# Attention over packed rows with a gated MLP: seven instead of six pairs of d_ff blocks go through a seven-product scheme

## The chip, the cores and the metric

The kernel runs on one core of a Trainium2 chip. TensorE (PE) multiplies matrices into PSUM, VectorE (DVE), ScalarE (ACT) and GpSimd (POOL) work elementwise, and SyncE's queue (SP) issues the DMAs. The metric is device time in microseconds (us), the median of several runs.

## The reference

For 8 batches of 8 heads, 32 packed rows `p` attend to 576 keys and values, and then 576 queries attend to the 32 packed results. The output, 4608 tokens by 512, goes through an MLP with d_ff = 2048. All is in fp32.

```
p_packed = sm_attn(p, k, v)
out = sm_attn(q, p_packed, p_packed)          # (8, 8, 576, 64)
x = out.transpose(0, 2, 1, 3).reshape(4608, 512)
h = x @ w_in                                  # (4608, 2048)
g = h * np.clip(h + 3.0, 0.0, 6.0) / 6.0
return g @ w_out                              # (4608, 512)
```

## The kernel before

**First product.** `x @ w_in` is never formed as it stands. Per batch a matrix m (256 by 2048) is made of the packed rows and `w_in`, and h = a m, where a holds the weights of the second softmax. Every fp32 operand is split into a high and a low part, and a product is three matmuls (high by high, high by low, low by high). For one d_ff block of 128 columns, `first_product` (L990) is six matmuls over the tokens of a chunk.

**Chunks.** A batch has two chunks of tokens, c = 0 and 1, written here as (b, c). One of them is narrow (256 tokens), one is wide (320). The 64 tokens on top go to a buffer `bnd` and are multiplied in the next odd batch as "edge" products.

**Second product.** Two d_ff blocks f and f+1 form a pair. Written as a 2 by 2 block product, the pair needs eight products of 128x128 by 128x256; `pair_product` (L1199) does it with seven, on sums of gate blocks (S1 to S4) and of weight blocks (T1 to T4): 21 matmuls of 256 columns. Four accumulators A, B, C, D hold the parts; after the last pair of a chunk, C and D are folded into the result by ACT (L1217), POOL (L1219) and three DVE instructions (L1222). The blocks that are not paired are multiplied one at a time (`single_product`, L1231): six matmuls of 512 columns for each block. At the end of a chunk two DVE instructions (L1236) add A and B and the store follows. From batch 2 on, six pairs and four single blocks make a chunk.

**Weight sums.** `combine` (L1126) makes T1, T2, T4 and T3 for a pair once, in batch 1. T3 overwrites a block of w_out, the other three go to SBUF slots (`wt`). The slots hold four pairs; pairs 0 and 4, and 1 and 5, share one, so they are kept in DRAM (`t_kept`, L1169) and fetched in turn (`fetch_t`, L1173), four fetches of 768 KB for each batch.

**Order.** A chunk walks over positions: all pairs first, then singles. At each half position `fill` (L1475) lets the attention of the next batch, its m and the fetches take the steps that the table STEPS names. A scheduler then orders each engine's instructions; a pair's or a single's second product stands one or two positions behind its first. PSUM has two buffers for h, so the first product of a position waits until the gate (L1009, DVE) two positions earlier has read its own.

Of the kernel before, what the change touches and what calls it, by code (L numbers as in the profile page):

```python
# [10 lines left out]
F32 = mybir.dt.float32  # L11
F32R = mybir.dt.float32r
# [24 lines left out]
    },  # L37
# [7 lines left out]
    },  # L45
# [7 lines left out]
    },  # L53
# [7 lines left out]
    },  # L61
# [7 lines left out]
    },  # L69
# [7 lines left out]
    },  # L77
    7: {
        "in": "",
        "pack": "",  # L80
        "ahead": "",
        "soon": "",
        "late": "2 4 6 8",
        "wt": "10 14 42 46",
    },
}


PAIRS = 6
FIRST_PAIRS = 4  # L90


# [42 lines left out]
def packed_attention_moe(  # L135
# [17 lines left out]
    nc = tc.nc  # L153
# [3 lines left out]
    P = 128  # L157
# [968 lines left out]
    def combine(i):  # L1126

        if i == 0:
            tiles = [wr.tile([P, 4, 2, H2], F32R, name=f"wt{n}", tag=f"w_in{n}") for n in (1, 2, 3)]
            for k, name in enumerate(("T1", "T2", "T4")):  # L1130
                for pair in range(PAIRS):
                    n, at = ((0, k), (1, k), (2, k), ((2, 0, 1)[k], 3))[pair % 4]
                    blocks[pair, name] = [tiles[n][:, at, x] for x in range(2)]
            for n in range(2):
                slots[n] = tiles[n].bitcast(F32)[:, :3]
        x, y = (xp.tile([P, W + P], F32, name="wx", tag="tb")[:, :H2] for _ in range(2))

        def whole(dst, name):
            hi, lo = (z.bitcast(F32) for z in block(i, name))
            nc.gpsimd.tensor_tensor(out=dst, in0=hi, in1=lo, op=ALU.add)  # L1140

        def kept(name, made):
            hi, lo = block(i, name)
            nc.scalar.copy(out=hi, in_=made)
            nc.vector.tensor_sub(out=lo, in0=made, in1=hi.bitcast(F32))

# [12 lines left out]
        nc.vector.tensor_add(out=x, in0=x, in1=lo)  # L1159
        kept("T2", x)  # L1160
        yield
        hi, lo = (z.bitcast(F32) for z in block(i, "B21"))
        nc.vector.tensor_sub(out=x, in0=hi, in1=x)
        nc.vector.tensor_add(out=x, in0=x, in1=lo)
        kept("T4", x)
        yield
        kept("T3", y)
        if i % 4 < 2:
            nc.sync.dma_start(out=t_kept[i % 4 + i // 4 * 2], in_=slots[i % 4].rearrange("p a x m -> p (a x m)"))  # L1169
        yield  # L1170

    def fetch_t(i):
        nc.sync.dma_start(out=slots[i % 4].rearrange("p a x m -> p (a x m)"), in_=t_kept[i % 4 + i // 4 * 2])  # L1173

    def moe_pairs(b, c, fill):

        pairs = list(range(FIRST_PAIRS if b == 1 else PAIRS))
        if c == 0:
            pairs.reverse()
        n_pairs = len(pairs)  # L1180
        steps = [2 * i + k for i in pairs for k in range(2)] + list(range(2 * n_pairs, NF))

        even = b % 2 == 0
        wide = (c == 1) == even
        n = 2 * P + REM if wide else 2 * P
        t0 = 0 if c == 0 else (2 * P if even else 2 * P + REM)
        off = REM if (wide and not even) else 0
# [6 lines left out]
        def bank(x):  # L1194
            if x not in banks:
                banks[x] = acc_of(roles["ABCD".index(x)])
            return banks[x]
# [30 lines left out]
                added(r2[:, :H2], 1, u1)  # L1228
                added(r2[:, H2:], 0, r2[:, :H2])

        def single_product(f, gh, gl):  # L1231
            for k, x in enumerate("AB"):
                second_product(f, bank(x), gh[:, k * P:(k + 1) * P], gl[:, k * P:(k + 1) * P], first=False)
                if f == NF - 1:
                    r = made["r"][k]
                    nc.vector.scalar_tensor_tensor(  # L1236
                        out=r, in0=bank(x), scalar=1.0 / 6.0, in1=r, op0=ALU.mult, op1=ALU.add
                    )
                    nc.sync.dma_start(out=out[row + k * P:row + (k + 1) * P], in_=r)
# [13 lines left out]
        for pos, f in enumerate(steps):  # L1253
            fill(pos)
            h = first_product(b, f, t0, n)
            if pos < 2 * n_pairs:
# [33 lines left out]
                fill(pos + 0.5)  # L1290
                second(1)
                continue
            t, gh, gl = gated(h, n, off)
            if wide:
                keep_edge(t, f, boff, 1 - even)
            if joined:
                while edges:
                    edges.pop(0)()
            pend.append(lambda f=f, gh=gh, gl=gl: single_product(f, gh, gl))
            fill(pos + 0.5)  # L1300
            second(2)
            if joined:
                j = f - 2 * n_pairs
                n_single = NF - 2 * n_pairs
                todo = [(2 * i, True) for i in range(n_pairs) if i * (n_single - 1) // n_pairs == j]
                if j == n_single - 1:
                    todo = [(g, False) for g in range(2 * n_pairs, NF, 2)]
                for g, summed in todo:
                    parts = edge_parts(g, summed)
                    edges.append(lambda g=g, summed=summed, parts=parts: edge_step(g, summed, parts))  # L1310
# [131 lines left out]
    xp = ctx.enter_context(tc.tile_pool(name="xp", bufs=2))  # L1442
    dram = ctx.enter_context(tc.tile_pool(name="dram", bufs=1, space=bass.MemoryType.DRAM))
    w_kept = dram.tile([NCH, P, FPC * DM], F32, name="w_kept")
    t_kept = dram.tile([PAIRS - 2, P, 3 * DM], F32, name="t_kept")

    def keep_w_in(n):
        nc.sync.dma_start(out=w_kept[n], in_=w_in_sb[n].rearrange("p f a e -> p (f a e)"))
# [13 lines left out]
    for b in range(1, B):  # L1462
# [2 lines left out]
        ahead = coarse(ahead)  # L1465
        if b == 1:
            late = coarse(part for n in range(1, NCH) for part in u_m(1, n))
            turned = [combine(i) for i in range(PAIRS)]
        else:
            late = coarse(u_m(b, NCH - 1))  # L1470
        soon = first_quarters(b + 1) if more else iter(())

        steps = {name: [int(x) / 2 for x in text.split()] for name, text in STEPS[b].items()}

        def fill(c, f):  # L1475
            s = c * NF + f
            with behind_gates():
                for _ in range(steps["late"].count(s)):
                    next(late, None)
                if b == 1:  # L1480
                    if s == 0:
                        with tc.issue_after(state["stored"].ins):
                            for n in range(NCH):
                                keep_w_in(n)
                    for i in range(PAIRS):
                        for _ in range(steps[f"t{i}"].count(s)):
                            next(turned[i], None)
                else:
                    for at, i in zip(steps["wt"], (1, 0, 4, 5)):
                        if s == at:  # L1490
                            fetch_t(i)
                for _ in range(steps["soon"].count(s)):
                    next(soon, None)
                if s == 31.5 and more:
                    rest(soon)
                    fetch_w_in(NCH - 1)
            done = state["out"] if b > 1 else state["load"]
            with tc.issue_after(state["load"].ins), tc.issue_after(done.ins), behind_gates():
                for chain, name in ((inputs, "in"), (packed, "pack"), (ahead, "ahead")):
                    for _ in range(steps[name].count(s)):  # L1500
                        next(chain, None)
                if s == 31.5:
                    rest(inputs, packed, ahead)
# [41 lines left out]
```

## Time and profile before

| | |
|---|---|
| median of 3 runs | 705.37 us (705.01 to 706.76) |
| profiled execution, first to last instruction (span) | 702.6 us |
| median less that span | 2.8 us |
| PE busy | 690.6 us, 98% of the span |
| DVE, ACT, POOL busy | 500.5, 428.7, 386.8 us |
| DMA: share of the 16 engines | 55.4% for the main queue |

The page gives no time of its own for the profiled execution but its span; what lies around it, start and end of the program, is taken as the 2.8 us by which the median is longer. A matmul's duration in the profile is its latency, since matmuls are pipelined; its cost is the distance between the starts of neighbours, which the chain of waits shows as a stretch of time with a count.

### The profile page before, as it was taken

How to read it: one execution, taken by the hardware profiler on the slowest of the kernel's cores; microseconds unless marked ns; L12 is line 12 of the kernel's file. 1: busy time of each engine (PE TensorE's matmuls, PEld its weight loads, DVE VectorE, ACT ScalarE, POOL GpSimd, SP SyncE). 2: the span in 40 equal slices, each digit the busy share in tenths (PEclk: the TensorE clock that was granted, in tenths of full speed). 3: DMA queues.
4: the chain of work that ended last, by engine and by line, in shares of the span. 5: the costliest groups of instructions: out<-in, count | busy, mean ns of one | idle time of the engine just before them, and what ended most of it. 6: DMA issues, size and time to landing. Idle time of an engine off the chain costs nothing.

```text
span 702.6 us, 16232 instructions
## 1 busy us (share of the span) xinstructions
PE 690.6 (98%) x5944; PEld 595.8 (85%) x5944; DVE 500.5 (71%) x1087; ACT 428.7 (61%) x1014; POOL 386.8 (55%) x620
## 2 busy tenths in 40 slices
PE   7899999999999999999999999999999999999997
PEld 5587877888979888898898988899898988989997
DVE  4898788768899669774687667876488766864443
ACT  4898886556656656564465655666366665755453
POOL 1556662545645565575554555566455646657563
PEclk9999999999999999999999999999999999999999
DMA  9989852983429665655446755483543835341030
GB/s 270 318 208 259 227 130 83 285 176 120 100 105 242 139 168 186 158 147 126 126 150 158 157 134 181 130 211 70 129 166 128 198 85 182 120 140 41 32 105 31
DMA packets 199104, 107.50 MB, mean 153 GB/s; under 512 B 173424, under 2 KB 185200, under 8 KB 195440
## 3 DMA queue, kind: packets, MB, share of 16 engines
q1 hardware_dynamic: 198480, 106.26, 55.4%
q8 instruction: 47, 0.77, 0.5%
q14 instruction: 33, 0.27, 0.1%
q10 hardware_dynamic: 544, 0.20, 0.1%
HBM read 89.65 MB, written 16.78 MB: 151 GB/s over the span
## 4 chain that ended last, share of the span: by engine, by line
PE 87%; DVE 6%; DMA 2%; ACT 2%; issue 1%; POOL 1%; SPq 0%; DVEq 0%; ACTq 0%
PE acc L1037 49%; PE ps_hh L997 24%; PE ps L413 6%; PE ps_h L670 3%; PE ps L1037 2%; PE ps L533 1%; DMA v_nat<-in_v_dram 1%; DMA room<-in_q_dram 1%; PE ps L503 1%; ACT t L1333 0%; DVE osb L1236 0%; SPq L706 0%; DVE t L1335 0%; PE ps L336 0%; DVE t L1009 0%
## 5 line engine op out<-in xcount | busy, mean ns | idle before, releaser
L997 PE MATMUL ps_hh<-a_hi,m_hi 128*128 128x320 f32 (+1 forms) x448 | 133.8, 299 | 0.4 <-PE acc L1037 0.3
L997 PE MATMUL ps_hh<-a_lo,m_hi 128*128 128x320 f32 (+1 forms) x448 | 132.9, 297 | 0.0
L997 PE MATMUL ps_hh<-a_hi,m_lo 128*128 128x320 f32 (+1 forms) x448 | 132.8, 296 | 0.0
L1009 DVE SCALAR_TENSOR_TENSOR t<-t,ps_hh 128x320 f32<-128x320 f32 (+1 forms) x148 | 66.0, 446 | 78.3 <-ACT t L1008 73.4
L1037 PE MATMUL acc<-wo_hi,g 128*128 128x512 f32 x288 | 103.4, 401 | 0.0
L1008 ACT ACTIVATE t<-ps_hh,three 128x320 f32<-128x320 f32 (+1 forms) x148 | 73.7, 500 | 44.8 <-PE ps_hh L997 39.3
L1015 POOL TENSOR_TENSOR gf<-tb,gf 128x256 fp32r<-128x256 f32 x76 | 62.3, 821 | 64.6 <-ACT gf L1014 57.9
L997 PEld LDWEIGHTS ps_hh<-a_hi,m_hi 128*128 128x128 f32 x448 | 84.7, 189 | 9.2 <-DVE t L1009 2.8
L997 PEld LDWEIGHTS ps_hh<-a_lo,m_hi 128*128 128x128 f32 x448 | 84.7, 189 | 4.4 <-issue 1.4
L997 PEld LDWEIGHTS ps_hh<-a_hi,m_lo 128*128 128x128 f32 x448 | 84.7, 189 | 2.2 <-issue 1.7
L1015 POOL TENSOR_TENSOR g<-t,g 128x256 fp32r<-128x256 f32 x72 | 55.1, 768 | 39.1 <-ACT g L1014 36.3
L1037 PE MATMUL acc<-wt,ga 128*128 128x256 f32 x456 | 74.4, 283 | 0.0
L1037 PE MATMUL acc<-wo_hi,ge 128*128 128x256 f32 x304 | 71.5, 285 | 0.0
L1037 PEld LDWEIGHTS acc<-wo_hi,g 128*128 128x128 f32 x288 | 52.8, 189 | 13.5 <-ACT g L1014 2.1
L1037 PEld LDWEIGHTS acc<-wt,ga 128*128 128x128 f32 x456 | 63.4, 190 | 0.7 <-issue 0.5
L1015 POOL TENSOR_TENSOR ga<-t,ga 128x256 fp32r<-128x256 f32 x76 | 60.5, 795 | 2.0 <-ACT ga L1014 1.8
L1037 PEld LDWEIGHTS acc<-wo_hi,ge 128*128 128x128 f32 x304 | 53.1, 190 | 6.6 <-issue 2.3
L1037 PE MATMUL acc<-wo_lo,g 128*128 128x512 f32 x144 | 56.8, 395 | 0.0
L618 DVE STREAM_TRANSPOSE tr<-nat 128x576 f32<-128x576 f32 x56 | 42.6, 767 | 18.2 <-DMA nat<-in_q_dram 8.8
L1008 ACT ACTIVATE tb<-ps_hh,three 128x256 f32<-128x256 f32 (+1 forms) x76 | 37.9, 499 | 26.5 <-PE ps_hh L997 24.9
L1279 POOL TENSOR_TENSOR tb<-tb,t 128x128 f32<-128x128 f32 x76 | 38.5, 507 | 27.4 <-DVE t L1274 26.7
L1033 POOL COPY bnd<-t 128x64 f32<-128x64 f32 x76 | 21.6, 284 | 55.1 <-DVE t L1009 54.9
(227 smaller groups left out, 1845.9 us busy)
## 6 DMA issues: line engine op xcount, KB each, us to landing
w_again<-w_kept SPq DMA_DIRECT2D x24, 1024.0 KB, 4.8
wt<-t_kept SPq DMA_DIRECT2D x24, 768.0 KB, 5.1
out_dram<-osb SPq DMA_DIRECT2D x33, 256.0 KB, 2.4
nat<-in_k_dram SPq DMA_DIRECT2D x112, 72.0 KB, 3.1
nat<-in_q_dram SPq DMA_DIRECT2D x112, 72.0 KB, 3.0
raw_in<-in_moe_w_in_dram SPq DMA_DIRECT2D x10, 512.0 KB, 6.1
raw_out<-in_moe_w_out_dram SPq DMA_DIRECT2D x10, 512.0 KB, 4.1
w_kept<-w_in_sb SPq DMA_DIRECT2D x4, 1024.0 KB, 7.5
```

The source lines that it names most:

```text
L413: nc.tensor.matmul(pair[x][NPK * a:NPK * a + NPK, :n], rows[half, a], c, start=True, stop=True)
L503: nc.tensor.transpose(out=pair[x][:, c * P:(c + 1) * P], in_=e[x][:, c * P:(c + 1) * P], identity=ident)
L533: nc.tensor.matmul(pair[x][cols, :D], l, r, start=(c == 0), stop=(c == NST - 1))
L618: nc.vector.transpose(out=t, in_=state.pop(("nat", which, b, a)))
L670: nc.tensor.matmul(h[:, hf, :HS], mm[:, g, fs], aa[:, hf * HS:(hf + 1) * HS], start=(g == 0 and i == 0), stop=(g == NG - 1 and i == 2),)
L997: state["first"] = nc.tensor.matmul(h[:, :n], mm[:, g, fs], aa[:, t0:t0 + n], start=(g == 0 and i == 0), stop=(g == NG - 1 and i == 2),)
L1008: state["relu"] = nc.scalar.activation(out=t[:, :n], in_=h, func=AF.Relu, bias=three)
L1009: state["gate"] = nc.vector.scalar_tensor_tensor(out=t[:, :n], in0=t[:, :n], scalar=6.0, in1=h, op0=ALU.min, op1=ALU.mult)
L1015: engine.tensor_sub(out=lo, in0=x, in1=hi.bitcast(F32))
L1033: nc.gpsimd.tensor_copy(out=bnd[:, f, side * REM:side * REM + REM], in_=t[:, boff:boff + REM])
L1037: nc.tensor.matmul(out, lhs[x], rhs[y], start=first and i == 0, stop=last and i == 2, skip_group_check=True)
L1279: nc.gpsimd.tensor_sub(out=s4, in0=b1, in1=s2)
```

## The change

PAIRS is 7. From (2, 1) on, eight chunks work seven pairs and two single blocks: (2,1), (3,1), (4,0), (4,1), (5,1), (6,0), (6,1), (7,1). The wide chunks of odd batches, (3,0), (5,0) and (7,0), keep six pairs; there the blocks 12 and 13, whose w_out block now holds a T3, are multiplied in two halves: block 13 uses its own gate on the left half and the sum of both gates on the right one. `combine` for pair 6 runs in batch 2. A third slot is shared (by pairs 2 and 6), so there are six fetches for each batch, and the order of the pairs within a chunk is new. The step tables of batches 2 to 7 are new.

```diff
 STEPS (batch 2, two of its lines; batches 3 to 7 are new too)
-        "wt": "12 13 44 54",
+        "wt": "12 14 36 42 46 50",
+        "wo": "25 28 28 28 33 33 33",
...
-PAIRS = 6
+PAIRS = 7
+SOFT_PAIRS = 6
+ORDER = ((5, 4, 3, 6, 1, 0, 2), (0, 1, 2, 3, 4, 5, 6))
+FETCHED = (1, 0, 2, 4, 5, 6)
...
-        if i % 4 < 2:
-            nc.sync.dma_start(out=t_kept[i % 4 + i // 4 * 2], in_=slots[i % 4]...)
+        if i % 4 < 3:
+            nc.sync.dma_start(out=t_kept[i % 4 + i // 4 * 3], in_=slots[i % 4]...)
...
+        wide = (c == 1) == (b % 2 == 0)
+        soft = b > 1 and wide and b % 2 == 1
+        n_pairs = FIRST_PAIRS if b == 1 else (SOFT_PAIRS if soft else PAIRS)
+        n_made = FIRST_PAIRS if b == 1 else PAIRS
+        if (b, c) == (2, 0):
+            n_pairs = n_made = SOFT_PAIRS
+        pairs = [i for i in ORDER[c] if i < n_pairs]
...
             for k, x in enumerate("AB"):
-                second_product(f, bank(x), gh[:, k * P:(k + 1) * P], gl[:, k * P:(k + 1) * P], first=False)
+                cols = slice(k * P, (k + 1) * P)
+                if whole is None:
+                    second_product(f, bank(x), gh[:, cols], gl[:, cols], first=False)
+                else:
+                    product(bank(x)[:, :H2], (gh[:, cols], gl[:, cols]), block(f // 2, "B21"))
+                    product(bank(x)[:, H2:], [z[:, cols] for z in whole], block(f // 2, "B22"))
...
+            if 2 * n_pairs < f < 2 * n_made and f % 2:
+                total = t[:, W:W + 2 * P]
+                nc.vector.tensor_add(out=total, in0=before[:, off:off + 2 * P], in1=t[:, off:off + 2 * P])
+                g3 = gp.tile([P, 4 * P], F32R, name="g3", tag="g", bufs=4)
+                split(g3[:, :2 * P], g3[:, 2 * P:], total)
...
+            turned = [combine(i) for i in range(SOFT_PAIRS, PAIRS)] if b == 2 else []
```

Line numbers move by four and more in the changed kernel: L1009 is L1013 there, L1037 is L1041, L1222 is L1230, L1236 is L1249.

**DVE, end of the program.** The first rows are the kernel before, the second the changed one. `osb` is the result being folded, `acc` an accumulator, `t` and `tb` gate blocks, `ge` a split gate block.

```order
L1015 TENSOR_TENSOR ge<-t,ge 128x256
L1009 SCALAR_TENSOR_TENSOR t<-t,ps_hh 128x256 x3
L1222 SCALAR_TENSOR_TENSOR osb<-acc,osb 128x256 x3
L1009 SCALAR_TENSOR_TENSOR t<-t,ps_hh 128x256
L1236 SCALAR_TENSOR_TENSOR osb<-acc,osb 128x512 x2
```

```order
L1019 TENSOR_TENSOR ge<-t,ge 128x256
L1013 SCALAR_TENSOR_TENSOR t<-t,ps_hh 128x256 x2
L1230 SCALAR_TENSOR_TENSOR osb<-acc,osb 128x256 x2
L1249 SCALAR_TENSOR_TENSOR osb<-acc,osb 128x512
L1230 SCALAR_TENSOR_TENSOR osb<-acc,osb 128x256
L1249 SCALAR_TENSOR_TENSOR osb<-acc,osb 128x512
```

The three folds stood ahead of the last gate; now no gate comes behind them, and the third one stands between the two instructions that finish A and B.

**SP, chunk (2, 1).** Before and changed again. `t_kept` is the DRAM copy of the weight sums, `wt` a slot, `w_again` a quarter of `w_in`, `nat` a piece of k or q of the batch after.

```order
L1239 DMA out_dram<-osb 128x512 x2
L357 DMA nat<-in_k_dram 32x18x32
L1452 DMA w_again<-w_kept 128x2048
L357 DMA nat<-in_k_dram 32x18x32 x6
L377 DMA p_nat<-in_p_dram 32x4x32 x4
```

```order
L1252 DMA out_dram<-osb 128x512 x2
L1173 DMA t_kept<-wt_1731 128x1536
L361 DMA nat<-in_k_dram 32x18x32
L1473 DMA w_again<-w_kept 128x2048
L361 DMA nat<-in_k_dram 32x18x32 x4
L1177 DMA wt_1731<-t_kept 128x1536
```

The sums of pair 6 are stored out of slot 1731, and then, five loads of k and one of `w_in` later, the sums of pair 2 are fetched into the same slot.

**PE, chunk (2, 1), the second product of pair 2.** Before and changed. `gf`, `ge` and `ga` are the split gate blocks of a pair, L413/L417 is a score product of the next batch's attention.

```order
L1037 MATMUL acc<-wt_1731,gf 128x256 x3
L1037 MATMUL acc<-wo_hi,ge 128x256
L1037 MATMUL acc<-wo_lo,ge 128x256
L1037 MATMUL acc<-wo_hi,ge 128x256 x2
L413 MATMUL ps_3709<-tr,pps 32x288 x8
L1037 MATMUL acc<-wo_lo,ge 128x256
L1037 MATMUL acc<-wo_hi,ge 128x256
L1037 MATMUL acc<-wt_1731,ga 128x256 x6
L1037 MATMUL acc<-wo_hi,ga 128x256
L1037 MATMUL acc<-wo_lo,ga 128x256
L1037 MATMUL acc<-wo_hi,ga 128x256
L997 MATMUL ps_hh<-a_hi,m_hi 128x320
```

```order
L1001 MATMUL ps_hh<-a_hi,m_hi 128x320
L417 MATMUL ps_3559<-tr,pps 32x288 x8
L1041 MATMUL acc<-wo_hi,ga 128x256
L1041 MATMUL acc<-wo_lo,ga 128x256
L1041 MATMUL acc<-wo_hi,ga 128x256
L1001 MATMUL ps_hh<-a_lo,m_hi 128x320
L1001 MATMUL ps_hh<-a_hi,m_lo 128x320
L1001 MATMUL ps_hh<-a_hi,m_hi 128x320
L1001 MATMUL ps_hh<-a_lo,m_hi 128x320
L1001 MATMUL ps_hh<-a_hi,m_lo 128x320
L1041 MATMUL acc<-wt_1731,gf 128x256 x3
L1041 MATMUL acc<-wt_1731,ga 128x256 x6
```

The nine matmuls that read slot 1731 stood ahead of the next first product; now they stand behind it.

## Rows read from the trace of the kernel before

**Rows 1.** The page's head: span, and busy time by engine.

```profile
span 702.6 us, 16232 instructions
PE 690.6 (98%) x5944; PEld 595.8 (85%) x5944; DVE 500.5 (71%) x1087; ACT 428.7 (61%) x1014; POOL 386.8 (55%) x620
```

**Rows 2.** Busy time by stretch: engines in us (x instructions), PEclk, DMA share, GB/s.

```profile
210.00:300.00 90.00, 89.67 (x805) 79.07 (x804) 70.47 (x155) 54.21 (x134) 50.15 (x89) 1.00 0.69 176
300.00:640.00 340.00, 340.00 (x3033) 300.78 (x3032) 239.92 (x529) 200.16 (x499) 191.12 (x337) 1.00 0.52 143
231.80:254.30 22.50, 22.50 (x237) 20.32 (x236) 13.79 (x38) 13.11 (x34) 11.69 (x21) 1.00 0.59 127
```

**Rows 3.** Who waited for whom, PE from 116 us on: us, times, longest.

```profile
PE ps_hh L997 <- PE acc L1037: 0.3, 1, 0.3
PE acc L1037 <- ACT wt L1144: 0.2, 1, 0.2
```

**Rows 4.** Chain of waits, 640 us to the end: start, us, what.

```profile
650.55 1.40 PE acc L1037 x6
...
652.95 1.39 PE acc L1037 x6
...
673.36 3.24 PE acc L1037 x27
...
685.57 2.47 PE acc L1037 x21
688.04 1.44 PE ps_hh L997 x12
...
694.79 3.45 PE acc L1037 x15
698.26 1.38 DVE osb L1236 x2
```

**Rows 5.** The page's groups: a weight load and POOL's part of a pair.

```profile
L1037 PEld LDWEIGHTS acc<-wt,ga 128*128 128x128 f32 x456 | 63.4, 190 | 0.7 <-issue 0.5
L1015 POOL TENSOR_TENSOR gf<-tb,gf 128x256 fp32r<-128x256 f32 x76 | 62.3, 821 | 64.6 <-ACT gf L1014 57.9
L1015 POOL TENSOR_TENSOR ga<-t,ga 128x256 fp32r<-128x256 f32 x76 | 60.5, 795 | 2.0 <-ACT ga L1014 1.8
L1279 POOL TENSOR_TENSOR tb<-tb,t 128x128 f32<-128x128 f32 x76 | 38.5, 507 | 27.4 <-DVE t L1274 26.7
```

**Rows 6.** Instructions in order of time, the folds at the end of (7, 1).

```profile
691.43 0.40 PE L1037 MATMUL acc<-wt,ga 128*128 128x256 f32 x2
691.66 0.28 PE L1037 MATMUL acc<-wo_hi,ga 128*128 128x256 f32 x1
691.86 0.60 ACT L1217 ACTIVATE osb<-acc 128x512 f32<-128x512 f32 x1 [0.93 <-PE acc L1037]
692.54 0.74 POOL L1219 TENSOR_TENSOR osb<-osb 128x256 f32<-128x256 f32 x1 [0.69 <-ACT osb L1217]
693.61 1.21 DVE L1222 SCALAR_TENSOR_TENSOR osb<-acc,osb 128x256 f32<-128x256 f32 x3
697.84 0.62 PE L1037 MATMUL acc<-wo_hi,g 128*128 128x512 f32 x2
```

**Rows 7.** Instructions in order of time, chunk (2, 1), DVE and PE.

```profile
246.09 0.43 DVE L1015 TENSOR_TENSOR ge<-t,ge 128x256 fp32r<-128x256 f32 x1 [0.47 <-ACT ge L1014]
249.17 0.49 DVE L1009 SCALAR_TENSOR_TENSOR t<-t,ps_hh 128x320 f32<-128x320 f32 x1 [0.45 <-ACT t L1008]
252.52 0.31 PE L997 MATMUL ps_hh<-a_hi,m_hi 128*128 128x320 f32 x1
263.57 0.31 PE L997 MATMUL ps_hh<-a_hi,m_hi 128*128 128x320 f32 x1
```

**Rows 8.** Groups by line, DVE's part of a combine, the longest and the shortest.

```profile
L1164 DVE TENSOR_TENSOR wx<-wx,wo_lo 128x256 f32<-128x256 f32 x6 | 4.5, 753 | 0.1
L1145 DVE TENSOR_TENSOR wo_lo<-wx,wo_hi 128x256 fp32r<-128x256 f32 x6 | 2.6, 430 | 0.0
```

**Rows 9.** Landing times of the DMAs on L1169, L1173 and L1448, in this order.

```profile
DMA to landing us min/median/max: 3.2/4.0/4.7
DMA to landing us min/median/max: 4.1/5.1/6.8
DMA to landing us min/median/max: 4.5/7.5/10.4
```

**Rows 10.** SP's queue in order of time, chunk (2, 1).

```profile
251.75 6.36 SPq L357 DMA_DIRECT2D nat<-in_k_dram  x6
```

More of the change, by code (lines that the diff above doesn't have):

```diff
@@ L82 @@
         "soon": "",
-        "late": "2 4 6 8",
-        "wt": "10 14 42 46",
-    },
-}
-PAIRS = 6
+        "late": "0 6 16 16",
+        "wt": "18 18 25 53 55 60",
+    },
+}
+PAIRS = 7
+SOFT_PAIRS = 6
+ORDER = ((5, 4, 3, 6, 1, 0, 2), (0, 1, 2, 3, 4, 5, 6))
+FETCHED = (1, 0, 2, 4, 5, 6)
 FIRST_PAIRS = 4
@@ L1133, in combine @@
                     blocks[pair, name] = [tiles[n][:, at, x] for x in range(2)]
-            for n in range(2):
+            for n in range(3):
                 slots[n] = tiles[n].bitcast(F32)[:, :3]
@@ L1167, in combine @@
         kept("T3", y)
-        if i % 4 < 2:
-            nc.sync.dma_start(out=t_kept[i % 4 + i // 4 * 2], in_=slots[i % 4].rearrange("p a x m -> p (a x m)"))
+        if i % 4 < 3:
+            nc.sync.dma_start(out=t_kept[i % 4 + i // 4 * 3], in_=slots[i % 4].rearrange("p a x m -> p (a x m)"))
         yield
     def fetch_t(i):
-        nc.sync.dma_start(out=slots[i % 4].rearrange("p a x m -> p (a x m)"), in_=t_kept[i % 4 + i // 4 * 2])
+        nc.sync.dma_start(out=slots[i % 4].rearrange("p a x m -> p (a x m)"), in_=t_kept[i % 4 + i // 4 * 3])
     def moe_pairs(b, c, fill):
[L1177 to L1180, printed above, removed]
+        wide = (c == 1) == (b % 2 == 0)
[5 more added lines that the diff above has]
+        pairs = [i for i in ORDER[c] if i < n_pairs]
+        if (b, c) == (2, 0):
+            pairs.sort(reverse=True)
         steps = [2 * i + k for i in pairs for k in range(2)] + list(range(2 * n_pairs, NF))
         even = b % 2 == 0
-        wide = (c == 1) == even
         n = 2 * P + REM if wide else 2 * P
@@ L1229, in pair_product, with single_product @@
                 added(r2[:, H2:], 0, r2[:, :H2])
-        def single_product(f, gh, gl):
+        def single_product(f, gh, gl, whole=None):
             for k, x in enumerate("AB"):
-                second_product(f, bank(x), gh[:, k * P:(k + 1) * P], gl[:, k * P:(k + 1) * P], first=False)
+                cols = slice(k * P, (k + 1) * P)
[4 more added lines that the diff above has]
+                    product(bank(x)[:, H2:], [z[:, cols] for z in whole], block(f // 2, "B22"))
                 if f == NF - 1:
@@ L1292, in moe_pairs @@
                 continue
+            before = made.get("t")
             t, gh, gl = gated(h, n, off)
+            made["t"], whole = t, None
+            if 2 * n_pairs < f < 2 * n_made and f % 2:
[3 more added lines that the diff above has]
+                split(g3[:, :2 * P], g3[:, 2 * P:], total)
+                whole = g3[:, :2 * P], g3[:, 2 * P:]
             if wide:
@@ L1298, in moe_pairs @@
                     edges.pop(0)()
-            pend.append(lambda f=f, gh=gh, gl=gl: single_product(f, gh, gl))
+            pend.append(lambda f=f, gh=gh, gl=gl, whole=whole: single_product(f, gh, gl, whole))
             fill(pos + 0.5)
@@ L1304, in moe_pairs @@
                 n_single = NF - 2 * n_pairs
-                todo = [(2 * i, True) for i in range(n_pairs) if i * (n_single - 1) // n_pairs == j]
+                todo = [(2 * i, True) for i in range(n_made) if i * (n_single - 1) // n_made == j]
                 if j == n_single - 1:
-                    todo = [(g, False) for g in range(2 * n_pairs, NF, 2)]
+                    todo = [(g, False) for g in range(2 * n_made, NF, 2)]
                 for g, summed in todo:
@@ L1444, in packed_attention_moe @@
     w_kept = dram.tile([NCH, P, FPC * DM], F32, name="w_kept")
-    t_kept = dram.tile([PAIRS - 2, P, 3 * DM], F32, name="t_kept")
+    t_kept = dram.tile([PAIRS - 1, P, 3 * DM], F32, name="t_kept")
     def keep_w_in(n):
@@ L1467, in packed_attention_moe @@
             late = coarse(part for n in range(1, NCH) for part in u_m(1, n))
-            turned = [combine(i) for i in range(PAIRS)]
+            turned = [combine(i) for i in range(SOFT_PAIRS)]
         else:
             late = coarse(u_m(b, NCH - 1))
+            turned = [combine(i) for i in range(SOFT_PAIRS, PAIRS)] if b == 2 else []
         soon = first_quarters(b + 1) if more else iter(())
@@ L1484, in fill @@
                                 keep_w_in(n)
-                    for i in range(PAIRS):
+                    for i in range(SOFT_PAIRS):
                         for _ in range(steps[f"t{i}"].count(s)):
@@ L1488, in fill @@
                 else:
-                    for at, i in zip(steps["wt"], (1, 0, 4, 5)):
+                    for part in turned:
+                        for _ in range(steps["wo"].count(s)):
+                            next(part, None)
+                    for at, i in zip(steps["wt"], FETCHED):
                         if s == at:
```

58 rows, old and new, of the table STEPS are left out of this document.

## The prediction

> **What bounds the kernel now.** I read the page's head first: PE is busy for 690.6 of 702.6 us, DVE for 500.5 [rows 1]. That is an average, so the windows came next: from 210 to 300 us PE is idle for 0.33 us, from 300 to 640 us for none, and DVE is busy there for 239.92 of 340 [rows 2]. The waits agree: from 116 us on the waits of PE for another engine are 0.3 and 0.2 us [rows 3]. So from there on the time is the length of PE's stream plus what follows its last matmul; a step that gets shorter on DVE, ACT or POOL gives nothing, and one that gets longer costs only where PE has to wait for it.
>
> The price of a matmul is its spacing, which the chain of waits gives over runs of neighbours [rows 4]. With 512 columns it is 1.40/6 = 0.233, 1.39/6 = 0.232 and 3.45/15 = 0.230 us. With 256 columns it is 3.24/27 = 0.120 and 2.47/21 = 0.118 us. Six first products of a narrow chunk take 1.44/2 = 0.72 us. The granted clock is 1.00, the level of 2.4 GHz, in all three windows [rows 2], so I need no second set of prices.
>
> **The change, part by part.** *PE's stream.* In eight chunks two single blocks become one pair: 12 x 0.232 = 2.784 us become 21 x 0.120 = 2.520 us. That is 0.264 us a chunk, 2.11 in all. Three chunks keep six pairs, and their blocks 12 and 13 are worked in halves: six matmuls of 512 become twelve of 256, 1.392 to 1.440, +0.05 each, +0.14 in all. In three odd chunks the edge products of the seventh pair also become twice as many at half the width, +0.07 in all. Net -1.90. With 0.230 and 0.118 it would be -2.2. I take -1.9, since the price of 0.120 comes from the longer run.
>
> At 256 columns the weight load is what could undo this. The matmul is 0.120 us apart from its neighbour although the profile gives a weight load 190 ns [rows 4, 5]: loads overlap one another, and the halved matmul still costs nearly half. The Trainium skill speaks against the change here: its page "TensorE: Matmul & The Clock Gate", section "Back-to-back issue gap", has the sustained spacing set by weight load and matmul together, about 81 ns at 128 columns and 131 ns at 512. Between these a straight line puts 256 columns at about 98 ns (an estimate from that page); a pair would be 21 x 0.098 = 2.05 against 12 x 0.131 = 1.57, and the eight chunks would lose about 3.8 us. The trace disagrees at both widths: 0.120 and 0.232, a ratio of 0.52.
>
> *The end of the program.* The change puts the seventh pair right before two singles in (7,1), so the folds of C and D, hidden before behind four singles, come within 12 matmuls of the end. From the start of C's last matmul (about 691.55, the second of the two at 691.43) to ACT it is 0.31 us, then ACT takes 0.60, POOL 0.74 after a gap of 0.08, and the three DVE folds 1.21/3 = 0.40 each [rows 6]. Placed after the change, with C's last matmul at zero: ACT ends at 0.91, POOL at 1.73, two folds at 2.61. A's last matmul is the ninth after it, at 9 x 0.229 = 2.06, and is done at 2.45. The finishing instruction for A, 1.38/2 = 0.69 [rows 4], then runs to 3.30, the third fold to 3.70, and the one for B to 4.39. That is 2.33 us after A's last start. Before it is 698.26 + 1.38 - 697.84 = 1.80 [rows 4, 6]. The end costs +0.5. It is 0.4 if only the one fold lies in the way, and 0.8 if both neighbours do.
>
> *Slot 1731 in (2,1).* This is the one new chain of waits that ends at PE. The sums of pair 6 are made in batch 2 (11 DVE instructions more, of 0.430 to 0.753 us by their group [rows 8], 5.7 us by the group means), stored from slot 1731, and the sums of pair 2 are fetched into it for a product that PE has in its stream right behind. DVE is busy for 13.79 of 22.5 us there [rows 2], so 8.7 us are free and the 5.7 fit. Two gates must not become late: six of the eleven fall between gates, 3.2 us, less the idle 0.47 and 0.45 in that place [rows 7], so the gate that ended at 249.17 + 0.49 = 249.66 ends at 252.0. PE's next first product starts at 252.52, half a microsecond later [rows 7]. Without that cover the price would be the size of the miss, some tenths; I take 0.
>
> The last write to the slot is at about 252.8. SP is in order, so the store goes out then and lands 4.0 us later [rows 9], at 256.8. Behind the store are five loads of k and one of w_again, at 6.36/6 = 1.06 each [rows 10]: the fetch issues at about 259.1, after the store has landed, and lands 5.1 us later [rows 9], at 264.2. The nine matmuls that read the slot stand behind a first product of the kind that started at 263.57 [rows 7]: there PE wants the slot at 263.57 + 0.88 (six of them at 0.147) - 9 x 0.120 = 263.4. The wait is 0.8 by the medians, none with the fastest fetch (4.1, 263.2), 2.5 with the slowest (6.8, 265.9). I take +0.5, between the first two, as SP may reach the fetch a load earlier. By the Trainium skill ("DMA: Bandwidth & Descriptors", section "Anatomy of one DMA — SWDGE (gpsimd) path"), a transfer takes 2.0 us plus its bytes over 436,000 per us, an estimate of 3.8 us for this one; the fetch would land at 262.9, PE would not wait, and the total would be 704.0. The trace has 4.0 and 5.1.
>
> *What costs nothing.* A seventh pair gives POOL two split sums and one gate sum more, 0.821 + 0.795 + 0.507 = 2.1 us [rows 5], against 3.96 us that PE needs for the pair (2.52 and two first products), with POOL at 191 of 340 us [rows 2]. The twelve more fetches use a queue with a DMA share of 0.52 [rows 2]. Slot 2 in an even batch is free after pair 6 and needed by pair 2 two pairs and six first products later, 2 x 2.52 + 6 x 0.72 = 9.4 us, against 6.8 for the slowest landing [rows 9]. If that cover is gone, at a landing of 10.4 as the slowest 1 MB stores [rows 9], it is 1.0 us in each of two batches. PE's order is unchanged up to the end of (2,0), so the 0.33 us of idle time stay.
>
> **Sum.** 702.6 - 1.9 + 0.5 + 0.5 = 701.7 us for the span of the profiled execution. Its own time I put at the median of 705.4, 2.8 us more than the span, so 704.5 us: 0.9 us, 0.13%, under the runs shown.
>
> **Rivals.** *The gain shows in full.* The spacing is 0.118, the fetch is in time, the third fold hides behind B's matmuls: 705.4 - 2.2 = 703.2, and 702.7 if the new steps also take the 0.5 us of waits away [rows 3]. For it: the prices of the fast rows. Against it: DVE's order at the end has the third fold between the two finishing instructions.
>
> *A late fetch turns into the bound.* Store and fetch of slot 1731 are serial, at a DMA share of 0.59 [rows 2]. If the store takes the 7.5 us of the median store on L1448, it lands at 260.3, the fetch goes out then, and with 6.8 us it lands at 267.1 [rows 9]: PE waits 3.7 us, and the time is 705.4 - 1.9 + 0.5 + 3.7 = 707.7. It decides against the change once the slot is full after 266.9. For it: in even batches the other fetches too have only 9.4 us. Against it: neither time was seen on the lines that move this size, and a store of 768 KB took 4.7 at most.
>
> *Weight loads set the pace.* If each matmul of 256 cost the 190 ns of its load, a pair would take 21 x 0.190 = 3.99 us, +1.2 a chunk, and the total would be about 714. The rows of 27 and 21 matmuls exclude it [rows 4].
>
> *The change does less than it says.* Three of the eleven chunks from (2,1) on keep six pairs. That is in the sum.
>
> **How the numbers follow.** 0.3%, 2.1 us, is about what a measurement of this kernel can tell from no change: faster is under 703.3, slower over 707.5. My forecast, and what lies between these bounds, has 0.60. The gain in full has 0.23: two of three things have to go well, and PE's rows leave little else to win. Slower has 0.17: 0.16 for fetches that come late, in (2,1) or in the even batches, since all step tables from batch 2 on are new, and 0.01 for the weight loads. The range is 702.7 to 707.7: its lower end is the full gain with the waits gone, its upper end the late fetch; about 0.06 lies below and 0.14 above.
>
> **What would show it.** Right: 21 matmuls of 256 at 0.118 to 0.120 where 12 of 512 were, in eight chunks; in (2,1) a wait of PE of under 1 us ahead of the nine matmuls from slot 1731, near 263 us; DVE's third fold between the two finishing instructions, and the last of them ending about 2.3 us after A's last start. Wrong: other lines in PE's list of waits, above all fetches in batches 4 and 6; a spacing of the new pairs far over 0.12; idle time of PE between 300 and 640 us, where there is none now.

## The result: slower, by 3 to 6.5 us

The changed kernel took 712.22 us (710.56 to 715.34, five runs) against 705.73 us (705.01 to 706.76) for the kernel before on the same chip: a ratio of 1.0086, interval 1.0058 to 1.0113. Timed again beside the kernel before (below, "again") it took 709.31 us against 706.28 us, a ratio of 1.0043 (1.0025 to 1.0060). Both times lie above the forecast of 704.5 us and above the range, which ended at 707.7 us.

The head of the profile after, of an execution of 715.34 us; it answers to [rows 1].

```profile
span 713.5 us, 16564 instructions
PE 695.1 (97%) x6043; PEld 604.4 (85%) x6043; DVE 517.3 (73%) x1128; ACT 437.7 (61%) x1040; POOL 405.4 (57%) x644
```

PE has 99 matmuls more and is still busy for 97% of the span, so this share does not show what was lost. The windows, in the columns of [rows 2]:

```profile
20.00:30.00 10.00, 8.85 (x113) 6.50 (x114) 6.22 (x15) 6.06 (x12) 3.93 (x3) 0.72 1.09 351
210.00:300.00 90.00, 88.81 (x799) 77.90 (x798) 76.72 (x171) 56.04 (x139) 54.48 (x90) 1.00 0.73 198
300.00:640.00 340.00, 336.40 (x3077) 300.26 (x3077) 245.60 (x547) 202.66 (x507) 197.18 (x345) 0.99 0.60 164
302.00:304.00 2.00, 0.34 (x3) 0.14 (x2) 2.00 (x4) 0.83 (x3) 0.99 (x4) 1.00 0.91 371
304.00:306.00 2.00, 1.62 (x19) 0.81 (x20) 0.24 (x1) 1.08 (x3) 1.66 (x3) 0.87 0.84 225
306.00:308.00 2.00, 2.00 (x11) 2.00 (x11) 1.16 (x2) 0.74 (x2) 0.00 (x0) 0.50 0.65 91
```

Between 300 and 640 us PE is now idle for 3.6 us, where it was never idle [rows 2], and the DMA share went from 0.52 to 0.60. One hole stands out, at 302 us, and behind it the granted clock is 0.50 for a while, the level of 1.2 GHz, so PE loses more than the wait itself. The longest entries in the list of PE's waits from 116 us on (in all, times, longest) tell what it waited for; they answer to [rows 3].

```profile
PE ps L417 <- DMA w_again<-w_kept: 2.0, 1, 2.0
PE acc L1041 <- ACT ga L1018: 1.5, 1, 1.5
PE acc L1041 <- DMA wt<-t_kept: 0.8, 1, 0.8
PE acc L1041 <- ACT wt L1148: 0.3, 1, 0.3
PE ps_hh L1001 <- PE acc L1041: 0.3, 1, 0.3
```

The last two were there before. The first is a quarter of `w_in` of 1 MB, a transfer that the change does not touch. SP's queue in order of time, and the matmul that waited:

```profile
293.21 1.95 SPq L361 DMA_DIRECT2D nat<-in_k_dram  x4
295.20 0.50 SPq L1252 DMA_DIRECT2D out_dram<-osb  x1
295.80 0.38 SPq L1473 DMA_DIRECT2D w_again<-w_kept  x1
296.23 0.44 SPq L1252 DMA_DIRECT2D out_dram<-osb  x1
299.32 0.32 SPq L1177 DMA_DIRECT2D wt<-t_kept  x1
```

```profile
304.38 1.09 PE L417 MATMUL ps<-w_again,pps 64*32 64x512 f32 x16 [2.03 <-DMA w_again<-w_kept]
```

Four loads of k and a store stand ahead of it, a store and a fetch of 768 KB behind it, at a DMA share of 0.9. PE wanted it 6.5 us after its issue, and it took 8.4 us to land. In the kernel before the same quarter was issued 5.9 us ahead of its use, with nothing in the queue beside it for its first 4 us; it landed after 4.8 us, in time:

```profile
284.52 0.32 SPq L1452 DMA_DIRECT2D w_again<-w_kept  x1
288.48 1.95 SPq L357 DMA_DIRECT2D nat<-in_k_dram  x4
```

```profile
290.39 1.09 PE L413 MATMUL ps<-w_again,pps 64*32 64x512 f32 x16
```

Landing times (min, median, max) of w_again and of the fetches after; before, they were 4.6, 4.8 and 7.0 for w_again.

```profile
DMA to landing us min/median/max: 4.7/5.2/8.7
DMA to landing us min/median/max: 4.1/5.2/8.3
```

By the Trainium skill ("DMA: Bandwidth & Descriptors", section "Anatomy of one DMA — SWDGE (gpsimd) path") 1 MB would be an estimate of 2.0 + 1,048,576/436,000 = 4.4 us. That section is on DMAs that GpSimd issues, and these are issued by SP. The trace's fastest, 4.7, is near the estimate; its slowest, 8.7, is not, and the estimate has no term for other transfers beside it.

The second wait is another transfer in disguise. Up to 481 us DVE stood at a transpose for loads of k; the sum of two gate blocks (L1287, DVE), its split on ACT (L1018) and PE were behind it in turn:

```profile
481.57 0.78 DVE L622 STREAM_TRANSPOSE tr<-nat 128x576 f32<-128x576 f32 x1 [2.34 <-DMA nat<-in_k_dram]
```

```profile
482.69 0.41 ACT L1018 CAST ga<-t 128x256 fp32r<-128x256 f32 x1 [2.81 <-DVE t L1287]
```

```profile
483.15 0.74 PE L1041 MATMUL acc<-wt,ga 128*128 128x256 f32 x4 [1.46 <-ACT ga L1018]
```

The third is slot 1731, which was forecast. These are the store, the loads and the fetch on SP, which answer to [rows 10], and the matmuls that waited:

```profile
257.60 0.33 SPq L1173 DMA_DIRECT2D t_kept<-wt  x1
...
259.89 0.53 SPq L1473 DMA_DIRECT2D w_again<-w_kept  x1
260.47 3.11 SPq L361 DMA_DIRECT2D nat<-in_k_dram  x4
263.68 1.48 SPq L1177 DMA_DIRECT2D wt<-t_kept  x1
```

```profile
269.56 0.62 PE L1041 MATMUL acc<-wt,gf 128*128 128x256 f32 x3 [0.76 <-DMA wt<-t_kept]
```

The stream itself did what was said. The chain of waits after answers to [rows 4]: 3.24/27 = 0.120 and 2.50/21 = 0.119 us with 256 columns, 1.40/6 = 0.233 with 512.

```profile
680.91 1.40 PE ps L1041 x6
...
683.94 3.24 PE acc L1041 x27
...
692.22 2.50 PE acc L1041 x21
```

And so did the end. C's last matmul starts at about 706.11 (the second of the two at 706.00, as in [rows 6]):

```profile
706.00 0.40 PE L1041 MATMUL acc<-wt,ga 128*128 128x256 f32 x2
```

The rows of ACT, POOL and DVE behind it:

```profile
706.43 0.60 ACT L1225 ACTIVATE osb<-acc 128x512 f32<-128x512 f32 x1 [0.96 <-PE acc L1041]
707.11 0.74 POOL L1227 TENSOR_TENSOR osb<-osb 128x256 f32<-128x256 f32 x1 [0.72 <-ACT osb L1225]
707.88 0.76 DVE L1230 SCALAR_TENSOR_TENSOR osb<-acc,osb 128x256 f32<-128x256 f32 x2 [2.85 <-POOL osb L1227]
708.62 0.69 DVE L1249 SCALAR_TENSOR_TENSOR osb<-acc,osb 128x512 f32<-128x512 f32 x1
709.22 0.42 DVE L1230 SCALAR_TENSOR_TENSOR osb<-acc,osb 128x256 f32<-128x256 f32 x1
709.74 0.69 DVE L1249 SCALAR_TENSOR_TENSOR osb<-acc,osb 128x512 f32<-128x512 f32 x1
```

From C's last matmul to the end of the last row it is 4.32 us, where 4.39 was worked out; from PE's last matmul to the end of the span 4.64 us, before 4.07.

One difference between the two traces does not come from the change. Batch 1 begins at 121.2 us after and at 116.7 before, though no engine's order differs up to there; between 20 and 30 us the clock was 0.72 after and 1.00 before. In the experiments the clock fell in that stretch in most profiles, in that of a kernel of six pairs too (0.83). Beside "again", six executions of the kernel before at a mean clock of 1.00 had spans of 702.6 to 704.8 us; on the chip of the last experiments one at 0.998 took 707.4. So 4.5 us of the 10.9 between the two profiled spans are the start of the program, not the change.

### The profile page after: what moved, and what is told of

It reads as the page before. It is cut to its first block, busy times and chain, and to the rows that moved or that the text cites. A ratio compares the mean times of both kernels' runs of the same rounds, so it can differ in the third digit from the quotient of the medians.

```text
span 713.5 us, 16564 instructions
## 1 busy us (share of the span) xinstructions
PE 695.1 (97%) x6043; PEld 604.4 (85%) x6043; DVE 517.3 (73%) x1128; ACT 437.7 (61%) x1040; POOL 405.4 (57%) x644
## 4 chain that ended last, share of the span: by engine, by line
PE 75%; DVE 5%; DMA 3%; SPq 1%; issue 1%; ACT 1%; POOL 1%; DVEq 0%; ACTq 0%
PE acc L1041 42%; PE ps_hh L1001 23%; PE ps L417 6%; PE ps L1041 2%; DMA w_again<-w_kept 1%; PE ps L537 1%; SPq L361 1%; DMA wt<-t_kept 1%; PE ps L507 1%; DMA nat<-in_k_dram 1%; PE ps_h L674 0%; DVE tr L622 0%; DMA nat<-in_q_dram 0%; DVE osb L1249 0%; DVE t L1013 0%
## 5 line engine op out<-in xcount | busy, mean ns | idle before, releaser
L1013 DVE SCALAR_TENSOR_TENSOR t<-t,ps_hh 128x320 f32<-128x320 f32 (+1 forms) x140 | 62.7, 449 | 81.6 <-ACT t L1012 77.9
L1019 POOL TENSOR_TENSOR gf<-tb,gf 128x256 fp32r<-128x256 f32 x84 | 68.9, 821 | 72.0 <-ACT gf L1018 65.6
L1041 PE MATMUL acc<-wt,ga 128*128 128x256 f32 x504 | 85.2, 287 | 1.5 <-ACT ga L1018 1.5
L1041 PE MATMUL acc<-wo_hi,g 128*128 128x512 f32 (+1 forms) x236 | 81.0, 387 | 0.2 <-ACT g L1018 0.2
L1041 PE MATMUL acc<-wo_hi,ge 128*128 128x256 f32 x336 | 80.6, 283 | 0.0
L1041 PEld LDWEIGHTS acc<-wt,ga 128*128 128x128 f32 x504 | 71.1, 192 | 9.0 <-issue 3.8
L1041 PEld LDWEIGHTS acc<-wo_hi,ge 128*128 128x128 f32 x336 | 59.5, 190 | 3.7 <-issue 1.9
L1292 POOL TENSOR_TENSOR tb<-tb,t 128x128 f32<-128x128 f32 x84 | 45.4, 540 | 26.6 <-DVE t L1287 25.4
L1019 POOL TENSOR_TENSOR g<-t,g 128x256 fp32r<-128x256 f32 x59 | 46.8, 798 | 18.9 <-ACT g L1018 18.0
L1018 ACT CAST ga<-t 128x256 fp32r<-128x256 f32 x84 | 34.2, 407 | 32.3 <-DVE t L1287 23.5
L1041 PE MATMUL acc<-wt,gf 128*128 128x256 f32 x252 | 52.3, 285 | 1.1 <-DMA wt<-t_kept 0.8
L1018 ACT CAST ge<-t 128x256 fp32r<-128x256 f32 x84 | 34.1, 406 | 29.0 <-DVE t L1278 25.2
```

What stands on the lines that cost most here:

```text
L1013: state["gate"] = nc.vector.scalar_tensor_tensor(out=t[:, :n], in0=t[:, :n], scalar=6.0, in1=h, op0=ALU.min, op1=ALU.mult)
L1018: nc.scalar.copy(out=hi, in_=x)
L1019: engine.tensor_sub(out=lo, in0=x, in1=hi.bitcast(F32))
L1041: nc.tensor.matmul(out, lhs[x], rhs[y], start=first and i == 0, stop=last and i == 2, skip_group_check=True)
L1292: nc.gpsimd.tensor_sub(out=s4, in0=b1, in1=s2)
```

## Experiments

Each kernel was timed against the kernel before on its own chip.

**again.** The changed kernel once more.

> The changed kernel once more, to see which of its losses come again. In its first profile it lost, against the kernel before: 4.5 us ahead of batch 1 (granted clock 0.72 between 20 and 30 us), 2.0 us of wait for w_again at 302 us and some 1.7 us of half clock behind it, 1.5 us at 481 us, 0.8 us at 268 us, 0.6 us at the end; the stream gave back 1.3. Theory A (late transfers): the time is 709 to 713 us again, and the waits at 268 and 302 us are there again, each over 0.5 us. Rival C (a clock lapse ahead of batch 1 that comes and goes, and is no matter of the change): when the granted clock is 1.00 up to batch 1, the time is within 2 us of the kernel before, 704 to 707.

1.0043 (1.0025 to 1.0060), 709.31 us. PE's longest waits:

```profile
PE ps L417 <- DMA w_again<-w_kept: 1.8, 1, 1.8
PE acc L1041 <- DMA wt<-t_kept: 0.8, 1, 0.8
PE acc L1041 <- ACT g L1018: 0.5, 1, 0.5
```

The waits for w_again and for slot 1731 came again, the one at 481 us did not. Three executions of again at a clock of 1.00 have spans of 704.9, 706.8 and 707.2 us against the 702.6 to 704.8 of the kernel before there, so rival C is out as the whole cause: some 3 us are lost at full clock too (means 706.3 and 703.2).

**no_extra.** The extra transfers alone are left out.

```diff
-                        if s == at:
+                        if s == at and i not in (2, 6):
...
-        if i % 4 < 3:
+        if i % 4 < 2:
```

> Leaves out the twelve fetches of the sums of pairs 2 and 6, and the two stores for them, so that pair 2 uses the sums of pair 6 from (2,1) on; the stream of PE is the same. Theory A (the extra transfers of 768 KB delay w_again, k and q): the waits at 268, 302 and 481 us go, and the time falls by 4 to 6 us, to 703 to 707. Rival B (the new step tables bunch the attention's steps, whatever is fetched): 710 to 712, waits at 302 and 481 us stay. Rival C: as the kernel again, 709 to 713, lost ahead of batch 1.

1.0023 (1.0002 to 1.0043), 708.29 us: 1.0 us under again by the medians, 1.4 by the ratios, less than theory A had and within the noise of the two. The executions at full clock tell them apart: three of no_extra at 0.999 and 1.00 have spans of 702.6 to 703.8 us, where those of the kernel before there lie between 702.3 and 704.8 and those of again between 704.9 and 707.2. In the profile, of an execution at 0.995, slot 1731 was waited for no more; w_again still was:

```profile
PE ps L417 <- DMA w_again<-w_kept: 1.8, 1, 1.8
```

So that wait does not need the twelve extra fetches: loads of k, two stores and a fetch of pair 5's sums, which stays, are enough beside it. Behind this hole the clock fell as well, to 0.50 between 302.5 and 304.5 us.

**old_steps and before_new_steps.** The tables crossed, for batches 2 to 7: before's `in`, `pack`, `ahead`, `soon` and `late` in the changed kernel, and the new ones in the kernel before. Two lines of batch 2, in old_steps:

```diff
-        "soon": "29 40 43 46 52 54 54 61 61 63 63 63",
-        "late": "12 14 19 29",
+        "soon": "36 47 47 47 47 49 51 52 52 53 53 53",
+        "late": "9 13 19 21",
```

> The changed kernel with the attention's steps of the kernel before in batches 2 to 7 (in, pack, ahead, soon, late), and its own steps for the fetches and for pair 6's sums. Theory A: the fetches are still in the way, other waits for transfers appear, and the time stays at 709 to 713. Rival B: the waits at 302 and 481 us go and no others come, 704 to 707. Rival C: no change, 709 to 713.

> The kernel before with the new tables for the attention's steps of batches 2 to 7, six pairs and four fetches a batch as before. Theory A: the bunched steps have room without the extra transfers, 704.5 to 707, within 1 us of the kernel before. Rival B: 3 to 6 us slower than the kernel before, 708 to 712, with waits for transfers near 302 and 481 us. Rival C: as the kernel before, 705 to 706.

old_steps: 1.0123 (1.0098 to 1.0148), 714.80 us, with three large kinds of waits. Two are for transfers, and the late gates are in part a third: at 398 us DVE had stood for 3.0 us for loads of k just ahead of the gate.

```profile
PE ps_hh L1001 <- DVE t L1013: 2.3, 3, 1.1
PE acc L1041 <- DMA wt<-t_kept: 2.3, 3, 0.9
PE ps L417 <- DMA w_again<-w_kept: 1.5, 1, 1.5
```

before_new_steps: 1.0048 (1.0029 to 1.0066), 709.63 us. PE's list has no transfer, but gates that came late. Ahead of the longer of the two, at 578 us, DVE had stood for 1.8 us for a load of q:

```profile
PE ps_hh L997 <- DVE t L1009: 0.9, 2, 0.7
```

No theory holds as a whole. In old_steps theory A had the pattern, with too short a time; in before_new_steps rival B had the time, with the waits elsewhere. Going back to the old tables does not mend the changed kernel, it is 5 us worse with them. Yet the new ones cost the kernel of six pairs 3 us, so new tables alone can lose as much as the change did; how much of its loss is theirs, these two runs do not tell. Here a table fitted one stream of PE and one set of transfers.

**late_2.** Meant to give w_again more time by a later step.

```diff
-        "late": "0 0 0 8",
+        "late": "2 2 2 8",
```

> One line of a table: the last quarter of m of batch 3 is worked one position later (late 2 2 2 8 in place of 0 0 0 8), so that w_again, issued near 294 us, has some 2.6 us more to land. Theory A (PE waits in line for transfers that come late, and the two waits in (2,1) are a good part of the loss): the wait of 1.8 us for w_again goes, and the time falls by 1.5 to 2.5 us against the changed kernel, to a ratio of 1.001 to 1.002 to the kernel before. Rival D (the wait only moves: something else, the fetch or a gate, is late by as much right behind): the ratio stays at 1.004.

1.0057 (1.0043 to 1.0072), 709.46 us; waits of 1.3 us for w_again and 1.4 for slot 1731. It tells nothing of the theory: no engine's order changed. The matmuls that read w_again stayed where they were, and only their PSUM buffer got another number. It counts as a second run of the changed kernel.

**late_no_extra.** no_extra with the same step.

> Leaves out the twelve fetches of the sums of pairs 2 and 6 and their two stores, as no_extra, and has the later step of late_2: seven pairs with neither of the two waits. Theory A: the stream's own gain shows, 1.9 less 0.5 at the end: 1 to 2 us under the kernel before, ratio 0.997 to 0.999. Rival E (the pairs of 256 columns or the new order of the attention's steps cost PE more than they give): the ratio is 1.000 to 1.003 with no wait of PE left over 0.5 us.

1.0024 (1.0009 to 1.0039), 708.04 us, wait for w_again 2.3 us: no_extra once more, for the same reason.

**slot_early.** Pair 6's sums are made earlier.

```diff
-        "wo": "25 28 28 28 33 33 33",
+        "wo": "23 26 26 26 31 31 31",
```

> One line of a table: pair 6's sums are made one position earlier, so that their store and the fetch of pair 2's sums go out ahead of the loads of k and of w_again. Theory A: the wait of 0.8 us for slot 1731 goes, 0.8 to 1.0 us less, ratio 1.003. Rival D: SP now stands at the fetch until the store has landed, w_again and k come later by some 4 us, and the time is the same or up to 2 us longer, ratio 1.004 to 1.007.

1.0054 (1.0037 to 1.0071), 709.72 us. The wait for slot 1731 is gone from the list, the one for w_again is 2.1 us. No gain can be seen; whether 0.8 us were won and lost again elsewhere is below what the interval can tell.

**mended.** late_2 and slot_early together, and six pairs in (7,1).

```diff
-        soft = b > 1 and wide and b % 2 == 1
+        soft = b > 1 and wide and b % 2 == 1 or (b, c) == (7, 1)
```

> The changed kernel with late_2 and slot_early together, and with six pairs in (7,1), so that the folds lie again behind four single blocks. Theory A: 1.8 + 0.9 + 0.3 us less than the changed kernel, ratio 0.999 to 1.001 to the kernel before. Rival D: 1.003 to 1.005. In the profile the end, from A's last matmul on, is 0.5 us shorter than in the changed kernel.

1.0072 (1.0056 to 1.0089), 710.25 us. From PE's last matmul to the end it is 4.22 us instead of 4.64, as expected; the time is not better: late_2 did nothing, and w_again was waited for again (1.8 us).

**soon_early.** The kernel that really moves w_again.

```diff
-        "soon": "29 40 43 46 52 54 54 61 61 63 63 63",
+        "soon": "29 38 41 44 48 50 52 57 58 60 60 60",
```

> One line of a table in batch 2 (soon): the quarters of w_in are worked some two half positions earlier, so that SP issues the last w_again ahead of the fetch of pair 5's sums, four loads of k and two stores, where in the changed kernel it stands behind them. late_2 did not move the matmuls that wait, so this is the first kernel that gives the transfer more time. Theory A (the wait of 1.3 to 2.3 us for w_again, seen in each kernel of seven pairs, comes from w_again's place in the queue): the wait falls under 0.3 us and the time by 1.5 to 2.3 us against the changed kernel, to a ratio of 1.002 to 1.003. Rival D (a wait of the same size takes its place): 1.004 to 1.006.

1.0043 (1.0026 to 1.0060), 709.63 us. The hole at the start of (3,0) is gone: SP issues that w_again some 5 us ahead of the loads of k and the stores,

```profile
284.98 0.32 SPq L1473 DMA_DIRECT2D w_again<-w_kept  x1
286.06 0.32 SPq L1177 DMA_DIRECT2D wt<-t_kept  x1
290.36 2.21 SPq L361 DMA_DIRECT2D nat<-in_k_dram  x4
```

but two other w_again were late, at 275 us (0.6) and at 442 us (1.3). Each was issued behind three fetches of 768 KB (two in soon_no_extra, where both were in time), as here for the second, which SP issued at 435.89:

```profile
428.78 3.46 SPq L1177 DMA_DIRECT2D wt<-t_kept  x3
```

```profile
PE ps L417 <- DMA w_again<-w_kept: 1.9, 2, 1.3
PE acc L1041 <- DMA wt<-t_kept: 0.7, 1, 0.7
```

Rival D holds in this execution: a wait of the same size took its place. Such waits differ between executions: in soon_tail, below, with the same order up to (7,1), the one at 442 us is absent.

**soon_no_extra.** The same without the extra transfers.

> Leaves out the twelve fetches of the sums of pairs 2 and 6 and their two stores, and has w_again early as soon_early: neither of the two waits. Theory A: the stream's gain less the longer end shows, ratio 0.997 to 0.999, PE's last matmul 1.5 to 2 us nearer to the start of batch 1 than in the kernel before (581.8 us there). Rival E (the pairs or the new order cost PE as much as they give): 1.000 to 1.003, with no wait of PE over 0.5 us left.

0.9995 (0.9979 to 1.0011), 706.48 us: level with the kernel before, and 3.4 us by the ratios below soon_early, from which only the twelve fetches and two stores differ. The two intervals do not overlap. Some of the 3.4 goes with the clock, which is 0.9976 in the mean here and 0.9965 in soon_early; a straight line through time and clock of the 71 executions of that session leaves 2.4 us at equal clock, give or take 0.9. Theory A and rival E both lie within the interval, so this run does not decide between them. No wait of PE for a transfer is left in its list. PE needs 582.5 us from batch 1's first matmul to its last, against 581.8 before; of these, 1.7 are waits for ACT and DVE that the kernel before did not have:

```profile
PE ps_hh L1001 <- DVE t L1013: 1.1, 1, 1.1
PE acc L1041 <- ACT g L1018: 0.6, 1, 0.6
```

The second is the wait in batch 1 that again shows too. The first is a transfer in disguise once more: DVE stood for 3.0 us for loads of k, and the gate behind it (L1013) came late for PE at 309.6 us.

```profile
309.49 0.78 DVE L622 STREAM_TRANSPOSE tr<-nat 128x576 f32<-128x576 f32 x1 [3.00 <-DMA nat<-in_k_dram]
```

So an old transfer can be late under the new tables without the extra ones. Without the two waits PE would need 580.8, a gain of 1.0 us, less than theory A had, of which the longer end takes 0.4.

**soon_tail.** soon_early with the end of mended.

> soon_early with six pairs in (7,1), so that the folds of C and D stand behind four blocks again. From PE's last matmul to the end it is 4.1 to 4.2 us as in the kernel before, not 4.6; the stream of (7,1) is 0.3 us longer, so the time is within 0.3 us of soon_early. Theory A: ratio 1.001 to 1.003. Rival D: 1.004 to 1.006.

1.0025 (1.0010 to 1.0040), 708.60 us. From PE's last matmul to the end it is 4.2 us, as in mended. It is the best of the kernels here that compute the whole, and still slower than the kernel before; its 1.0 us under soon_early are within the noise of the two.

**soft_all.** Six pairs in every chunk, with the transfers and tables of seven.

```diff
-        soft = b > 1 and wide and b % 2 == 1
+        soft = b > 1
```

> The changed kernel with all its transfers and tables, but six pairs in every chunk from (2,1) on: blocks 12 and 13 are worked one at a time everywhere (13 in halves), so that PE has 72 matmuls of 256 columns less and 48 of 512 more. By the spacings of 0.119 and 0.232 us that is 2.5 us more of stream in the eight chunks. Theory A (the stream's gain is real, and the loss lies in the transfers): 1.5 to 3 us slower than the changed kernel, ratio 1.006 to 1.009. Rival E (seven pairs do not pay): the same time as the changed kernel or less, 1.002 to 1.005.

In (4,0) and (6,0) pairs 0 and 2 now come ahead of the fetch of their sums and are multiplied with those that the slot still holds; the work is the same. 1.0113 (1.0088 to 1.0138), 714.56 us: 5 us over again, more than the 2.5 us of the stream. The waits changed as well, with three for w_again (2.7 us) where the changed kernel had one. In the two profiles PE needs 4.6 us more than in again from batch 1's first matmul to its last (588.9 and 584.3); summing each start against the usual spacing, 1.9 of it are waits and slips, and what is left, 2.7, is near the 2.5. So the seventh pair seems to shorten PE's stream as forecast; one profile of each kernel is all that stands behind it.

## Why the prediction was wrong

- **PE's stream, -1.9.** Right in size. PE has 123 matmuls of 512 columns less and 222 of 256 more; at the measured 0.2315 and 0.1195 us that is -28.47 + 26.53 = -1.9. About half of it does not arrive: other starts between neighbours slip by 0.1 us in some more places, 0.9 us in again's profile by summing each start against the usual spacing. No run shows why.
- **The end, +0.5.** Right: +0.57 (4.64 less 4.07), and the third fold stands where it was said.
- **Slot 1731, +0.5.** The mechanism was right, the place too; the size was 0.8 us in the first profile and in again, 1.4 in late_2. Batch 1 began 4.5 us later in the first profile than in the kernel before; with that taken off, SP reached the fetch at 259.2, where 259.1 was worked out, and PE wanted the slot at 264.3, where it was 263.4. What was longer is the landing: 5.8 us in the place of the median of 5.1 (5.8 in again, 6.8 in late_2).
- **"What costs nothing" is the step that failed.** It charged nothing for the twelve more fetches because the queue's share was 0.52 [rows 2], and asked only whether the new transfers arrive in time. The old ones do not: in the changed kernel w_again was waited for in each of three executions (2.0, 1.8, 1.3 us), and in one of them k as well. Its slack could have been read before: 5.9 us from issue to use, with a landing of 4.8 in the median and 7.0 at most. The share of 0.52 is a mean over 340 us; in the changed kernel, at the place where it counted, it was 0.9. What shows the cause are soon_early and soon_no_extra, which differ by the extra transfers alone: 1.0043 against 0.9995, 3.4 us, or 2.4 at equal clock. In soon_early's profile these are waits of 1.9 us for w_again and 0.7 for slot 1731; with both gone the kernel is level with the one before, not under it.
- **The new step tables** had a place among the chances, but no term in the sum. In before_new_steps they cost the kernel of six pairs 3 us. They also bring old transfers closer to their use: no quarter of w_in had less than 5.9 us from issue to use in the kernel before, and in again two have 4.9, at 461 and 627 us, and land 0.2 us ahead of their use. Whether the place of w_again in the queue is a second cause is not shown: without the extra transfers the early place is 2.0 us better by the ratios (no_extra 1.0023, late_no_extra 1.0024, soon_no_extra 0.9995), but these ran on three chips, and the two slower ones at a lower mean clock (0.9968 against 0.9976), part of which can be the fall behind the hole. With the extra transfers, moving it gives nothing that can be measured (again and soon_early both 1.0043).
- **The rival "a late fetch turns into the bound"** was the right side, with the wrong transfer: I had the chain through slot 1731 at 3.7 us, and it gave 0.8 to 1.4; the rest came through transfers that I had not put on the list. The fetches in the even batches, which the rival also feared, were in time.
- **"The gain shows in full" and the weight loads** are out: the spacing is 0.119 to 0.120. Two sums there are off, without effect: with the fast rows the stream gains 2.1 us, not 2.2, and at 190 ns for each matmul the eight chunks alone would give 715 us, not 714.
- **From span to time, 2.8 us.** In each execution whose span is on record, time and span are 1.7 to 2.3 us apart. About 1 us of the 2.8 is the spread between executions; it does not explain the miss.

For again, in us, PE's part from batch 1 on: -1.9 (stream) + 1.9 (w_again) + 1.0 (slot 1731, by starts) + 0.6 (a wait in batch 1, which only some profiles show) + 0.9 (small slips) = +2.5, where the starts give 584.3 - 581.8 = +2.5; with 0.6 at the end, +3.1. The ratio of 1.0043 is +3.0.

What stays open: the first five executions were 6.5 us slower than the kernel before, the later ones 3.0 (again) and 3.6 (late_2). The first profile has two items that again's lacks, the wait at 481 us (1.5) and 1.5 us lost to the half clock behind the hole at 302 us, but whether the other four executions had them can't be told. Two of those four ran at 0.998 and 0.999 and still have spans of 709.2 and 708.7 us, so the clock alone is not the answer.

## What to carry to other kernels

Where PE is the bound and idles nowhere, list for every transfer that PE or DVE waits for the time from issue to use and the slowest landing, the old transfers first: here a change that added traffic was paid for by transfers with little slack, most of them not its own. Follow late gates back as well: several here stood behind DVE waiting for k or q. The mean DMA share did not tell of this; read it in the two or three microseconds around the use. And a table of steps is part of the stream that it was made for: crossed with another, it lost 3 to 5 us here in either direction.

## What the runs showed of the hardware

Seven profiles have a hole of 1.3 to 2.3 us in PE's stream at the same place, the start of (3,0). In two of them, the first one after the change (2.0 us) and no_extra (1.8), it was followed by a granted clock of 0.50, the level of 1.2 GHz, and by first products 0.26 us apart instead of 0.147: from the first of the late matmuls to the 120th behind it took 14.9 us, where the other five needed 13.4. So the fall cost 1.5 us on top of the wait. In the others the clock stayed at 1.00, behind longer holes too (2.1 us in slot_early, 2.3 in late_no_extra); what decides it is not seen. Ahead of batch 1, where no kernel here changes an order, batch 1 starts at 116.7 to 117.6 us in the three profiles with a clock of 1.00 between 20 and 30 us, and at 118.2 to 121.2 us in the eleven with 0.67 to 0.84 there. PE was busy for 8.4 to 9.0 of these 10 us either way, so what tips the clock is not seen. This spread of 4.5 us is more than the change costs at full clock, and one profile of each kernel would have charged it to the change.
